# Two engines share the last rows, and all engines get new sequences: a one-core mix of a state-space convolution and a spectral filter

## The chip, the cores and the metric

The kernel runs on one core of one Trainium2 chip. The metric is device time in microseconds (us) of one execution, as the median of the timed runs. The engines are named as in the profile: PE is TensorE's matmuls and PEld its weight loads, DVE is VectorE, ACT is ScalarE, POOL is GpSimd, SP is SyncE, which here only issues DMAs. A `q` behind an engine's name (ACTq, SPq) means its instruction queue, for instance the issue of a DMA.

## What is computed

Two branches over 2048 positions and 640 channels are mixed by a gate for each position. Branch A convolves `u` along the positions with a kernel `K` that is a sum of 128 complex exponentials for each channel (computed by FFT in the reference). Branch B multiplies the two-dimensional spectrum of the same input by weights:

```
x = A_u
g = sigmoid((x * gate_w).sum(-1, keepdims=True))
a = irfft(rfft(u, 4096) * rfft(K, 4096))[:2048] + u * D_skip      # K = 2 Re sum_n C exp(A dt l)
b = irfft2(rfft2(x) * (w_r + 1j * w_i))
return g * a + (1 - g) * b
```

## The kernel before

All transforms are matmuls in float32 against tables, in stages of short transforms. The 640 channels are worked in four blocks `c` of 160.

- **Phase A** (`phase_a`, L575 to L643) transforms `u` (matmuls L532 and L546), writes the spectrum to HBM (`u_d`) and makes the gate.
- **The spectral filter** (the second half of `phase_a`, L659 to L782) reads that spectrum back in nine pairs of frequencies: transposes (L700), products with tables (L710, L764), the elementwise filter on VectorE, copies out of PSUM on ScalarE (L702, L717, L753, L768), and writes `s3e_d`.
- **Phases P and B** (L427 to L883) make the convolution kernel K in 40 tiles of 16 channels: matmuls L832 and L840, on ScalarE an exponential (L833) and two sines (L846 outer, L852 inner), products on VectorE (L860 to L862) and GpSimd (L865, L866), matmuls L876, a copy L882 and a write to `k_d`. Exponential and sine need different ScalarE tables; a tiny activation at L409 (`PRIME`) is put where the function changes, so that the table load stands there.
- **Phases C and D** (L876 to L1052) transform K (L532, L546), multiply with the spectrum of `u` (`us`, loaded at L960; L971 to L974), transform back (L988, copies L990 and L992), write the result to HBM (`s3_d`, for the last block `s3f_d`; issued by ScalarE's queue at L997 and L1000), load it back in another layout (`t3`, L1021 by SyncE), and make the last transform (`last`, L1030).

The last stage of a block has three chunks of 3, 3 and 2 rows (`CHUNKS`) for each of two halves `j`: 16 rows of 160 channels on 128 partitions. `last_e` makes branch B's part, times (1 - g), into `oe`. `last_c` makes branch A's part in PSUM, multiplies by g and adds `oe` into `ot`; the output leaves from `ot` (L1052). In the last block (`c == 3`) each row is one VectorE instruction (L1048) that multiplies and adds. Before these, eight matmuls at L1072 whose result nobody reads keep TensorE running. For the last block, `t3` is loaded in twelve pieces: four sets of partitions `y` (`t3[y::4]`), each of three chunks. Set 3 holds the last group of frequencies (written at L1000); set 2 needs also the odd frequency (written at L997).

The order of all work is written out by hand: the program is recorded as a numbered list of operations, and `ORDER` lists the numbers (`5846+10` is 5846 to 5855). Each engine runs its own operations in that order and waits where it must; DMAs are issued by the engine on which they are listed. Buffers are given to tiles in the same order. Numbers that matter below: 5787 to 5794 are the last eight matmuls of L988, 5795 is the copy behind them, 5796 and 5797 the last two writes at L1000, 5749 and 5750 those at L997. 5826 to 5837 are the twelve loads (three each for sets 0, 1, 2, 3). 5846 to 5853 is the first chunk's block of L1030 matmuls.

Two sorts of operations have no result that is used: `SPARE` is a count of fill matmuls (L406, 128 columns each), which the order puts where TensorE would stand still, and `PRIME` is the count of the tiny activations by function (Exp, Sin, Arctan, Ln, Sigmoid).

Of the kernel before, what the change touches and what calls it, by code (L numbers as in the profile page):

```python
# [15 lines left out]
ALU = mybir.AluOpType  # L16
# [926 lines left out]
def phase_d(tc, A, T, ctx, out):  # L943
# [95 lines left out]
    def last_c(c, a, n):  # L1039

        oe = oes.pop((c, a))
        p = last("p_c", lambda g: T.e3[c < 3], lambda g, r: t3s[c][r, 4 * a + n * g:4 * a + n * g + n], n)
        ot = o2.tile([128, 2, 3, 160], F32, tag="ot", name="ot")
        if c == 3:
            for j in range(2):
                for i in range(n):
                    x = 8 * j + a + i
                    V.scalar_tensor_tensor(out=ot[:, j, i], in0=p[:, j, i], scalar=T.gate[:, 0, x:x + 1], in1=oe[:, j, i], op0=ALU.mult, op1=ALU.add)  # L1048
        else:
            V.tensor_tensor(out=ot[:, :, 0:n], in0=p, in1=gate(0, a, n), op=ALU.mult)  # L1050
            G.tensor_tensor(out=ot[:, :, 0:n], in0=ot[:, :, 0:n], in1=oe[:, :, 0:n], op=ALU.add)
        (G if c < 2 else nc.sync).dma_start(out[c].rearrange("p (j a) d -> p j a d", j=2)[:, :, a:a + n], ot[:, :, 0:n])  # L1052
# [24 lines left out]
SPARE = (128, 278), (32, 0)  # L1077
PRIME = 23, 23, 1, 1, 1
# [97 lines left out]
```

## Time and profile before

| | |
|---|---|
| three timed runs | 535.62, 536.0, 543.41 us; median 536.0 |
| the profiled execution | 533.92 us, its span 531.9 |
| granted TensorE clock, mean | 0.993 |
| DMA moved in the span | 101.17 MB, 190 GB/s |
| TENSOR_TENSOR of VectorE in the last 36 us, 128x640 from PSUM (L971) | 0.82 us each |
| outputs issued by SyncE after 510 us (L1052) | 6, 3.0 to 4.8 us from issue to landing |

The profile's rows give the line, the engine, the operation, what it writes and reads, the shape and the count, then busy us and mean ns of one, then the idle time of the engine before them and what ended it. A row of a stretch (from:to) gives its length, the busy us of each engine with the number of instructions, the granted TensorE clock, the share of DMA time and GB/s. A float32 matmul leaves two records. A row of a chain or of a timeline begins with the start and the length in us.

### The profile page before, as it was taken

The numbers are of one execution on the slowest core, as the hardware profiler recorded it, in microseconds if no ns is written. First come the engines' busy times: TensorE is split into PE (matmuls) and PEld (weight loads), VectorE is DVE, ScalarE is ACT, GpSimd is POOL, SyncE is SP. The second block draws the span as 40 slices with busy tenths as digits, with TensorE's granted clock in tenths as the row PEclk, the third lists the DMA queues.
The fourth block names the chain that finished last, engine by engine and source line by source line (L and its number), as shares of the span: only waits on it lengthen the run. The fifth ranks groups of instructions, "written<-read, shape, count | busy, mean of one in ns | idle before, by whom it ended". The sixth has DMA issues, their size and how long they took to land. (4 is left out here: it accounts for less than half of the span.)

```text
span 531.9 us, 19458 instructions
## 1 busy us (share of the span) xinstructions
PE 499.3 (94%) x8600; PEld 409.5 (77%) x8600; DVE 397.6 (75%) x548; ACT 354.6 (67%) x505; POOL 226.1 (43%) x236
## 2 busy tenths in 40 slices
PE   8999999899999989999989999998999997999993
PEld 6899797788887878877768888886797886887740
DVE  5994236989899999598688696879575673767754
ACT  3787887699989877899969989966433242332210
POOL 1003213674766253746554525526431245337350
PEclk9999999999999999999989999999999999999998
DMA  8969526782313335132040231413997799799986
GB/s 318 361 199 339 171 81 215 250 256 84 101 67 110 125 103 170 46 118 70 30 147 32 67 110 52 127 55 123 358 338 240 247 374 390 261 321 311 340 266 234
DMA packets 58363, 101.17 MB, mean 190 GB/s; under 512 B 4980, under 2 KB 42136, under 8 KB 58248
## 3 DMA queue, kind: packets, MB, share of 16 engines
q1 hardware_dynamic: 34680, 67.82, 37.2%
q10 hardware_dynamic: 20368, 21.79, 12.3%
q0 software_dynamic: 3232, 10.33, 5.8%
q8 instruction: 67, 1.10, 0.8%
q14 instruction: 16, 0.13, 0.1%
HBM read 60.60 MB, written 39.65 MB: 188 GB/s over the span
## 5 line engine op out<-in xcount | busy, mean ns | idle before, releaser
L546 PE MATMUL psum<-sbuf,sbuf 128*64 128x160 f32 x1056 | 89.2, 308 | 6.5 <-ACT sbuf L536 2.7
L546 PEld LDWEIGHTS psum<-sbuf,sbuf 128*64 128x64 f32 x1056 | 72.7, 134 | 19.3 <-issue 6.5
L406 PE MATMUL psum<-sbuf 128*128 128x128 f32 x556 | 79.0, 287 | 0.0
L532 PE MATMUL psum<-sbuf,sbuf 128*64 128x128 f32 x1280 | 77.2, 274 | 0.2 <-issue 0.2
L406 PEld LDWEIGHTS psum<-sbuf 128*128 128x128 f32 x556 | 67.0, 192 | 11.3 <-issue 9.1
L532 PEld LDWEIGHTS psum<-sbuf,sbuf 128*64 128x64 f32 x1280 | 72.2, 137 | 3.8 <-issue 2.5
L710 PE MATMUL psum<-sbuf 64*128 64x161 f32 (+1 forms) x864 | 68.9, 305 | 4.3 <-DVE sbuf L771 2.2
L710 PEld LDWEIGHTS psum<-sbuf 64*128 64x128 f32 (+1 forms) x864 | 60.8, 182 | 9.4 <-DVE sbuf L771 2.3
L862 DVE TENSOR_TENSOR sbuf<-sbuf,psum 128x1024 f32<-128x1024 f32 x40 | 48.5, 1216 | 25.3 <-ACT psum L852 25.2
L833 ACT ACTIVATE sbuf<-psum 128x1024 f32<-128x1024 f32 (+1 forms) x80 | 60.9, 803 | 4.8 <-PE psum L832 3.1
L409 ACT ACT_TABLE_LOAD x48 | 61.6, 1283 | 0.8
L974 POOL TENSOR_TENSOR sbuf<-sbuf 128x320 f32<-128x320 f32 (+1 forms) x36 | 32.1, 893 | 68.3 <-DVE sbuf L972 57.3
L990 ACT COPY sbuf<-psum 128x640 f32<-128x640 f32 x32 | 21.9, 693 | 52.3 <-PE psum L988 36.1
L865 POOL TENSOR_TENSOR sbuf<-sbuf,sbuf 128x512 f32<-128x512 f32 x24 | 34.0, 1417 | 31.2 <-ACT sbuf L846 22.4
L579 ACT COPY sbuf<-psum 128x512 f32<-128x512 f32 (+2 forms) x58 | 35.3, 626 | 17.1 <-PE psum L532 11.7
L536 ACT COPY sbuf<-psum 128x512 f32<-128x512 f32 x40 | 23.9, 620 | 34.2 <-PE psum L532 22.8
L852 ACT ACTIVATE psum<-psum 128x1024 f32<-128x1024 f32 x40 | 40.3, 1008 | 9.3 <-PE psum L840 9.2
L876 PEld LDWEIGHTS psum<-sbuf 128*32 128x32 f32 x2560 | 37.9, 110 | 9.1 <-issue 7.1
L876 PE MATMUL psum<-sbuf 128*32 128x64 f32 x2560 | 44.4, 221 | 0.5 <-issue 0.4
L988 PEld LDWEIGHTS psum<-sbuf,sbuf 64*128 64x128 f32 x528 | 37.6, 186 | 6.8 <-issue 4.6
L988 PE MATMUL psum<-sbuf,sbuf 64*128 64x160 f32 x528 | 42.7, 305 | 0.1
L846 ACT ACTIVATE sbuf<-psum 128x1024 f32<-128x1024 f32 x40 | 40.7, 1017 | 2.8 <-PE psum L840 2.8
(133 smaller groups left out, 827.9 us busy)
## 6 DMA issues: line engine op xcount, KB each, us to landing
u_d<-sbuf SPq DMA_DIRECT2D x32, 320.0 KB, 4.2
sbuf<-u_d ACTq DMA_DIRECT2D x16, 640.0 KB, 6.7
s_d<-sbuf ACTq DMA_DIRECT2D x24, 320.0 KB, 5.8
sbuf<-s_d SPq DMA_DIRECT2D x6, 960.0 KB, 8.4
sbuf<-in_w_l SPq DMA_DIRECT2D x8, 644.0 KB, 4.1
sbuf<-u_d SPq DMA_DIRECT2D x8, 640.0 KB, 4.8
k_d<-sbuf SPq DMA_DIRECT2D x20, 256.0 KB, 2.3
sbuf<-k_d SPq DMA_DIRECT2D x8, 640.0 KB, 6.9
```

The source lines that it names most:

```text
L406: nc.tensor.matmul(spare[x:x + cols, i, :], c1[:, x:x + cols], c1[:, 128:256], start=True, stop=True)
L409: nc.scalar.activation(prime[0:1, i:i + 1], c1[0:1, 0:1], f)
L532: nc.tensor.matmul(p[64 * ri:64 * ri + 64, q // 4, 0:512].rearrange("p (h x) -> p h x", h=2)[:, :, 64 * (q % 4):64 * (q % 4) + 64], src[:, ...
L546: nc.tensor.matmul(p[64 * j:64 * j + 64, y, 160 * ro:160 * ro + 160], T.w2[:, x, ro, :], t1[:, x // 2 if x < 32 else K0 // 2, :, x % 2 if ...
L579: return (V.tensor_copy if T.dve and dst.home.name == "ut" else S.copy)(dst, src)
L710: P.matmul(p[:st.nl, c, 161 * i:161 * i + 161], src[r, k, x, 0:st.nl], td[r, w, k, :], start=k == 0, stop=k == 2)
L833: S.activation(ef[:, :, c:c + n], p[:, :, 0:n], AF.Exp)
L846: S.activation(sc.rearrange("p d v i -> p (d v i)"), p.rearrange("p j w -> p (j w)"), AF.Sin, scale=TWO_PI)
L852: S.activation(f, f, AF.Sin, scale=TWO_PI)
L862: V.tensor_tensor(out=x[:, 0].rearrange("p d (h j) -> p d h j", h=2), in0=e[:, :, 0:64].rearrange("p d (h j) -> p d h j", h=2), in1=cx.uns ...
L876: P.matmul(st.pb[32 * r:32 * r + 32, o, :], y[:, ri, 4 * qq + r, :], x[:, ri, 4 * qq + r, :], start=t % 2 + qq + 1 - ri == 0, stop=t % 2 * ...
L988: P.matmul(p[:, j, 160 * i:160 * i + 160], T.w3[r, pr, im, :], t2[r, h + i, im], start=im == 0, stop=im == 1)
```

## The change

In the last block, rows `i` = 0 and 1 of the second half `j` = 1 of each chunk, six of the 16, no longer run on VectorE. ScalarE multiplies them by the gate on the way out of PSUM (an activation with a scale for each partition), and GpSimd adds `oe`. Ten rows stay on VectorE.

```diff
@@ -1045,7 +1045,11 @@
             for j in range(2):
                 for i in range(n):
                     x = 8 * j + a + i
-                    V.scalar_tensor_tensor(out=ot[:, j, i], in0=p[:, j, i], scalar=T.gate[:, 0, x:x + 1], in1=oe[:, j, i], op0=ALU.mult, op1=ALU.add)
+                    if j and i < 2:
+                        S.activation(ot[:, j, i], p[:, j, i], AF.Copy, scale=T.gate[:, 0, x:x + 1])
+                        G.tensor_tensor(out=ot[:, j, i], in0=ot[:, j, i], in1=oe[:, j, i], op=ALU.add)
+                    else:
+                        V.scalar_tensor_tensor(out=ot[:, j, i], in0=p[:, j, i], scalar=T.gate[:, 0, x:x + 1], in1=oe[:, j, i], op0=ALU.mult, op1=ALU.add)
         else:
             V.tensor_tensor(out=ot[:, :, 0:n], in0=p, in1=gate(0, a, n), op=ALU.mult)
             G.tensor_tensor(out=ot[:, :, 0:n], in0=ot[:, :, 0:n], in1=oe[:, :, 0:n], op=ALU.add)
```

`SPARE` has 64 fill matmuls less and `PRIME` one sine less. `ORDER` is replaced as a whole:

```diff
-SPARE = (128, 278), (32, 0)
-PRIME = 23, 23, 1, 1, 1
+SPARE = (128, 214), (32, 0)
+PRIME = 23, 22, 1, 1, 1
...
-5682 5695+8 5570 5568 5673 5704 5683+8 5703 5706 5691 5707+8 5705 5693 5828 5692 5715 5799+8 5827 5826 5716 5740+2 5717+10 5743 5742 5745 5744 5728+8
-5727 5807 5746+2 5736 5752+8 5738 5737 5748 5761 5760 5764+8 5763 5571+8 5762 5773 5776+8 5772 5775 5774 5784 5829 5831 5579 5582+8 5786 5830 5787+8
-5785 5590 5580 5795 5593+8 5808+8 5750 5601 5796+2 5838+8 5602 5816 5749 5581 5591 5603 5835 5832 5836 5833 5837 5592 5834 5817+9 5846+10 5861+8 5857
-5856 5859 5858 5869 5860 5873 5870 5872 5876+8 5871 5874 5885 5875 5886+2 5884 5888
...
+5628 5447+2 5627 5650+8 5449 5637 5751 5658 5638+8 5659 5646 5662+8 5660+2 5647+2 5671 5674+8 5568 5670 5673 5570 5682 5695+8 5569 5672 5703 5799+8
+5704 5707+8 5807 5706 5827 5683+8 5705 5826 5715 5828 5719+8 5691 5717 5716 5693 5740+2 5727 5718 5692 5743 5571+8 5742 5745 5744 5752+8 5579 5761
+5580 5808+8 5760 5728+8 5762+2 5736 5764+8 5581 5816 5737+2 5582+8 5772+2 5746+2 5590 5829 5776+8 5775 5748 5830+2 5774 5591 5784 5593+8 5817+8 5785
+5601 5786+9 5749+2 5602 5825 5592 5795+2 5838+8 5797 5603 5832+6 5846+9 5863+8 5859 5855 5857 5860+2 5856 5858 5874 5880+8 5876 5871 5875 5862 5888
+5892 5890 5889 5893 5872 5891 5873 5878 5877 5894 5879
```

Up to 5856 the numbers mean the same in both. In the new list each of the six rows is two operations (ScalarE, then GpSimd: 5857 and 5858, 5859 and 5860 for the first chunk; 5873 to 5876 for the second, 5890 to 5893 for the third), the second chunk's matmuls are 5863 to 5870 and the third's 5880 to 5887, its outputs are 5862, 5879 and 5894, the fill is 5895 to 6108 (before: 5889 to 6166) and the tiny activations 6109 to 6156 (before: 6167 to 6215). Every engine's sequence changes, in the middle of the kernel too. In the end shown here, the old order of the last loads is 5835 5832 5836 5833 5837, an output (5592), 5834; the new one is 5592 and 5603, then 5832 to 5837 in order of number. The old order has three blocks of L1030 before 5787 that the lines above show from 5799 on; the new one has six.

135 rows, old and new, of the table ORDER are left out of this document.

## The prediction

> **What bounds the kernel now.** I read the page first, then the busy times by stage, then the last stage's chain and timeline. The profiled execution took 533.92 us around a span of 531.9; the three timed runs have a median of 536.0. I make the sum on the former and carry the difference over.
>
> ```profile
> span 531.9 us, 19458 instructions
> PE 499.3 (94%) x8600; PEld 409.5 (77%) x8600; DVE 397.6 (75%) x548; ACT 354.6 (67%) x505; POOL 226.1 (43%) x236
> ...
> L406 PE MATMUL psum<-sbuf 128*128 128x128 f32 x556 | 79.0, 287 | 0.0
> ...
> L409 ACT ACT_TABLE_LOAD x48 | 61.6, 1283 | 0.8
> ```
>
> TensorE (PE) looks full, but L406 is fill: 278 matmuls (two records each) of 79.0/278 = 0.284 us that no result uses. They stand where the sequence expects TensorE to wait. So the middle of the kernel must be read for ScalarE and TensorE together. I cut it at every fourth inner activation (L852, tiles 1, 5, 9 ... 37 and the last):
>
> ```profile
> core 0: us, PE busy (x) PEld busy (x) DVE busy (x) ACT busy (x) POOL busy (x), PEclk, DMA share, GB/s
> 76.70:113.70 37.00, 34.83 (x562) 27.93 (x559) 30.07 (x34) 29.16 (x39) 16.75 (x16) 1.00 0.67 221
> 113.70:147.50 33.80, 33.03 (x616) 27.59 (x616) 31.00 (x37) 32.84 (x45) 23.29 (x23) 1.00 0.38 123
> 147.50:167.60 20.10, 19.12 (x376) 15.86 (x374) 19.49 (x27) 17.55 (x24) 11.51 (x12) 1.00 0.29 98
> 167.60:215.70 48.10, 46.38 (x768) 38.41 (x768) 46.98 (x63) 37.10 (x50) 22.05 (x26) 1.00 0.39 119
> 215.70:237.30 21.60, 20.98 (x488) 16.78 (x485) 15.78 (x20) 21.23 (x29) 11.77 (x11) 1.00 0.25 79
> 237.30:261.90 24.60, 23.88 (x404) 19.18 (x403) 19.12 (x27) 23.68 (x33) 13.60 (x13) 1.00 0.17 55
> 261.90:290.70 28.80, 25.63 (x466) 20.87 (x464) 24.18 (x29) 24.67 (x35) 17.04 (x18) 0.94 0.28 87
> 290.70:315.70 25.00, 24.06 (x482) 19.78 (x480) 18.42 (x24) 23.53 (x33) 8.26 (x8) 1.00 0.21 69
> 315.70:361.60 45.90, 45.26 (x802) 38.11 (x798) 36.48 (x49) 37.94 (x54) 22.96 (x20) 1.00 0.31 92
> 361.60:374.10 12.50, 10.37 (x266) 7.97 (x268) 11.48 (x15) 7.74 (x11) 7.21 (x10) 1.00 0.36 119
> sum 297.40, PE 283.53 PEld 232.47 DVE 252.99 ACT 255.44 POOL 154.43; mean PE 28.35 PEld 23.25 DVE 25.30 ACT 25.54 POOL 15.44
> ```
>
> ScalarE is 94 to 98% busy in four of the ten stretches (the second, fifth, sixth, eighth) and idles in the others: 37.00 - 29.16 = 7.8 us in the first, 11.0 in the fourth, 8.0 in the ninth. After that come the convolution's stages, where TensorE and the DMA engines are full, and the end:
>
> ```profile
> 379.70:494.00 114.30, 110.22 (x1632) 92.96 (x1630) 75.26 (x109) 37.49 (x61) 45.26 (x49) 1.00 0.90 316
> 494.00:511.00 17.00, 15.53 (x208) 11.20 (x212) 13.28 (x19) 3.54 (x6) 6.63 (x7) 1.00 0.98 321
> ```
>
> Of the 131 us there TensorE idles 5.6. The matmuls in these stages are the same in both sequences, so a new order can win little in them. The last 20 us are a chain of waits:
>
> ```profile
> 509.56 0.59 ACTq L1000
> ...
> 510.19 0.73 ACTq L1000
> ...
> 511.74 1.19 ACTq L1000
> ...
> 512.97 4.40 DMA s3f_d<-sbuf
> ...
> 518.11 0.57 SPq L1021
> ...
> 523.86 1.04 PE psum L1030 x16
> ```
>
> The last write to HBM lands at 512.97 + 4.40 = 517.37 (call it W). Then SyncE issues the last six reloads, the three chunks' matmuls follow, then VectorE's rows and the last output:
>
> ```profile
> 517.45 3.17 SPq L1021 DMA_DIRECT2D sbuf<-s3f_d  x5
> 520.66 0.60 SPq L1052 DMA_DIRECT2D out<-sbuf  x1
> 521.31 0.62 SPq L1021 DMA_DIRECT2D sbuf<-s3f_d  x1
> 521.33 1.04 PE L1030 MATMUL psum<-sbuf,sbuf 64*32 64x480 f32 x16 [1.55 <-DVE sbuf L1037]
> 524.93 3.08 DVE L1048 SCALAR_TENSOR_TENSOR sbuf<-psum,sbuf,sbuf 128x160 f32<-128x160 f32 x10 [0.69 <-PE psum L1030]
> 525.89 0.77 PE L1030 MATMUL psum<-sbuf,sbuf 64*32 64x320 f32 x16 [0.99 <-issue]
> 528.04 0.53 SPq L1052 DMA_DIRECT2D out<-sbuf  x1
> ```
>
> The chunks start at W + 4.0, + 6.5 and + 8.5, the last output is issued at W + 10.7 and the span ends at W + 14.5. A row costs VectorE 3.08/10 = 0.31 us.
>
> **The change, part by part. The last rows.** Six rows leave VectorE: 6 x 0.31 = 1.85 us of its 4.9. Each becomes an activation from PSUM and a GpSimd add. Nearest rows:
>
> ```profile
> L992 ACT COPY sbuf<-psum 64x160 f32<-64x160 f32 x1 | 0.3, 287 | 1.5 <-PE psum L546 1.5
> L974 POOL TENSOR_TENSOR sbuf<-sbuf 64x160 f32<-64x160 f32 x1 | 0.5, 517 | 0.0
> L974 POOL TENSOR_TENSOR sbuf<-sbuf 128x320 f32<-128x320 f32 x4 | 3.6, 908 | 8.2 <-DVE sbuf L972 8.2
> ```
>
> So 0.29 us on ScalarE, and 0.52 on GpSimd, whose upper bound is the 320-wide 0.91. I take 0.52, the row of the same 160 elements. The per-row scale is not in the copy's row; its bounds are nothing and a second 0.29, and ScalarE has only six rows to make while VectorE makes ten, so nothing. In the new order the two adds of the second and third chunk queue on GpSimd behind each other, and the last two outputs on SyncE wait for them; nothing waits behind those.
>
> **The last reloads.** The old order interleaves partitions "3" and "2" of each chunk and puts an output (5592) ahead of the last load. The new one issues the three loads of "2" first. They need only the writes up to L997, which now go out ahead of the last two L1000, so they can land before W. After W remain three loads, at about W + 0.1, + 0.7 and + 1.3 (one per 0.63 us in the row of five) instead of six up to W + 3.9. Before, the first chunk's second load was issued at 518.11 and its matmuls began at 521.33, 3.2 us later; the third chunk's came 525.89 - 521.31 = 4.6 us after its last load. With 3.1 to 4 us from issue to matmuls, since fewer loads fly together, the chunks can start at W + 3.2, + 4.3 and + 5.3. VectorE's four rows of chunk one run W + 4.3 to 5.5, then it waits for chunk three at W + 6.1, and ends near W + 7.9; ScalarE ends at W + 6.9; GpSimd, six adds of 0.52 from W + 4.7 with short waits, at W + 8.2. The last output goes at W + 8.3 instead of + 10.7: 2.4 us won. With 0.91 per add GpSimd ends at W + 10.2 and 0.4 is won.
>
> **What is put ahead of W.** Before the last eight L988 matmuls the new order has six L1030 blocks where the old had three:
>
> ```profile
> L1030 PE MATMUL psum<-sbuf,sbuf 64*32 64x480 f32 x96 | 6.2, 571 | 4.4 <-DVE sbuf L1037 1.6 <-DMA sbuf<-s3f_d 1.5 <-DMA sbuf<-s_d 1.4
> L1030 PE MATMUL psum<-sbuf,sbuf 64*32 64x320 f32 x48 | 2.3, 440 | 1.0 <-issue 1.0
> ```
>
> A block of 16 records is 6.2/6 = 1.04 us or 2.3/3 = 0.77. One long and two short ones are 2.6 us more. They cover the 1.4 us wait on the s_d reload, so W comes 1.2 later; the first L1000 after the last copy took 1.19 where the two before it took 0.59 and 0.73, and without an L997 still to come behind it I give 0.5 back. W moves by +0.7 (between 0 and +2.6), and the end of the kernel wins 2.4 - 0.7 = **1.7 us** (-2.2 to +2.4).
>
> **Table load.** PRIME has one Sin less, so one pair of load and tiny activation goes: 1.28 + 0.20 us.
>
> ```profile
> 208.52 1.28 ACT L409 ACT_TABLE_LOAD   x1
> ...
> 209.82 0.20 ACT L409 ACTIVATE sbuf<-sbuf 1x1 f32<-1x1 f32 x1
> ```
>
> It counts by ScalarE's busy share of the ten stretches, 255.44/297.40 = 0.86: **1.3 us** (0 to 1.5). The Trainium skill (ScalarE: Activation LUTs, What ACT_TABLE_LOAD costs) adds a drain of 1380 ns to each load. Here the activation starts 0.02 us after the load, so no drain shows behind it; by the page this term would be (1.28 + 1.38 + 0.20) x 0.86 = 2.5 us, an estimate, and the sum below 7.5.
>
> **Fill and order in the middle.** Counted between the same L852 in both sequences, the fill changes by -12, -14, -4, -16, +9, -7, -12, +5, -15, +2 (sum -64), 18.2 us of TensorE. F-stage work (L700, L710, L764) per tile stays the same to within 24 instructions, so the mix of stages hardly moves. A stretch can shorten by no more than its removed fill, and by no more than ScalarE's idle time in it. In the four full stretches that gives 1.0 - 2.5 + 0.9 - 1.4 = -2.0 us. In the other six at most 3.4 + 1.1 + 4.5 + 3.4 + 4.2 - 0.6 = 16.0. Both ends: none of it, or 14.0 in all. The long fill runs stand where ScalarE is full (131 of 278 in the four stretches, 105 of 297 us), and in the idle stretches ScalarE waits mostly for real matmuls; so I take a third of the 16.0: 5.3 - 2.0 = **3.3 us** (-2.0 to 14.0).
>
> **Sum:** 1.7 + 1.3 + 3.3 = 6.3 us. 533.92 becomes 527.6 as profiled, and 536.0 becomes **529.7** as timed.
>
> **The rivals.** *A really shorter middle.* If removed fill means that real work moved up, all 14.0 us come: 14.0 + 1.3 + 1.7 = 17.0, 519.0 us. For it speak 297.4 - 255.4 = 42 us of idle ScalarE; against it the unchanged mix. It is past 2% from 10.7 - 3.0 = 7.7 us in the middle.
>
> *The clock falls (the other side).* Less fill leaves TensorE idle:
>
> ```profile
> 268.70:272.10 3.40, 1.22 (x18) 1.09 (x20) 3.39 (x5) 2.50 (x4) 2.38 (x4) 1.00 0.28 77
> 272.10:275.50 3.40, 3.40 (x28) 2.78 (x25) 2.00 (x2) 0.75 (x1) 0.00 (x0) 0.50 0.87 211
> ```
>
> A stretch with 1.22 us of work in 3.40 was followed by 3.4 us at clock 0.50, which costs 1.7 us. Suppose the middle gains nothing from its order and the clock falls in five more places: 536.0 - 1.7 + 5 x 1.7 = 542.8 us. It decides from the second place on. Against it: 18.2 us spread over 300 is one fill in 4.7 us, and the old kernel fell only once. The Trainium skill (TensorE: Matmul & The Clock Gate, Why this matters for your kernels) wants a gap of about 3 us before the clock drops; by that this rival costs nothing. The rows disagree: 2.2 us idle sufficed.
>
> *The end gains nothing* (GpSimd adds at 0.91, or W later by all 2.6 us): 536.0 - 4.6 = 531.4.
>
> **How the numbers follow.** Forecast 0.42 (its own range, with -1 to +7.4 us from the middle, 525.6 to 534), shorter middle 0.30, clock 0.18, no gain at the end 0.10. A measurement tells about 2%, 10.7 us. The shorter middle is past it (0.30 faster); the clock rival is past it from eight places on, for which I keep 0.10; the rest, 0.42 + 0.10 + 0.08 = 0.60, is within. The range is 519.0 to 541.0: down to the whole of the first rival, up to four falls of the clock.
>
> **What would show it.** Right: the last output about 8.3 us after the last s3f_d write lands, VectorE's rows no longer last, GpSimd adds near 0.52; the last L876 some 4 to 5 us sooner; clock 1.00 in the middle but for a place or two. Wrong: an s3f_d reload issued after W waiting on L997, adds near 0.9, several rows of clock 0.5 to 0.8, or a middle shorter by over 8 us.

## The result, and the profile after

The kernel after takes 541.47 us, the median of 20 runs (537.34 to 547.92), against 536.52 for the kernel before in 20 runs beside it. The ratio is 1.0103, with a 95% interval of 1.0077 to 1.0129: slower by 1.0%, which is less than 2%, but the interval excludes no change. The time lies 0.5 us past the upper end of the range. (Ratios leave disturbed runs out, so one can differ a little from the quotient of two medians.) The profiled execution took 543.57 us around a span of 541.6, 9.7 us more than that of before, where the medians lie 4.95 apart. Much of what follows is about that difference.

The head of the page and the two rows of fill and table loads, as shown of before:

```profile
span 541.6 us, 19212 instructions
PE 489.8 (90%) x8472; PEld 400.2 (74%) x8472; DVE 399.5 (74%) x542; ACT 355.1 (66%) x509; POOL 227.4 (42%) x242
...
L406 PE MATMUL psum<-sbuf 128*128 128x128 f32 x428 | 64.2, 291 | 0.0
...
L409 ACT ACT_TABLE_LOAD x47 | 60.3, 1283 | 0.8
```

The work went as announced: 14.8 us less fill, one table load less, and TensorE busy for 9.5 us less in a span that is 9.7 us longer. So TensorE stands still for 19 us more in this execution. Its longest waits in the first 400 us of after (us in total, times, longest):

```profile
PE psum L832 <- DMA sbuf<-par_d: 3.8, 1, 3.8
PE psum L876 <- DVE sbuf L860: 2.5, 2, 2.1
PE psum L840 <- DVE sbuf L773: 2.4, 2, 2.2
...
PE psum L876 <- issue: 2.2, 1, 2.2
PE psum L532 <- DMA sbuf<-in_u_l: 2.1, 1, 2.1
PE psum L700 <- DVE sbuf L579: 2.1, 1, 2.1
```

Before had one wait of 2 us or more there (2.2 us, L710 on VectorE's L771), and its first L832 waited 1.2 us for the same DMA. Five stretches of 3.4 us that hold a wait from this list, each with the stretch behind it (from:to, length, busy us of each engine, granted clock, DMA share, GB/s):

```profile
59.20:62.60 3.40, 1.25 (x20) 1.03 (x22) 0.00 (x0) 1.31 (x3) 0.00 (x0) 1.00 0.40 96
62.60:66.00 3.40, 3.40 (x36) 3.15 (x32) 0.00 (x0) 0.81 (x2) 0.00 (x0) 0.51 0.00 0
103.60:107.00 3.40, 1.38 (x17) 1.19 (x18) 3.40 (x4) 1.64 (x3) 2.55 (x3) 1.00 0.87 311
107.00:110.40 3.40, 3.40 (x25) 2.03 (x22) 3.40 (x6) 1.07 (x2) 1.79 (x2) 0.50 0.75 237
236.70:240.10 3.40, 1.25 (x64) 1.00 (x55) 3.40 (x5) 2.54 (x4) 0.30 (x1) 1.00 0.62 236
240.10:243.50 3.40, 3.40 (x70) 2.55 (x60) 2.38 (x4) 1.91 (x3) 0.00 (x0) 0.51 0.15 61
277.70:281.10 3.40, 1.30 (x12) 1.09 (x12) 3.40 (x6) 1.87 (x3) 1.85 (x3) 1.00 0.13 39
281.10:284.50 3.40, 3.40 (x56) 2.65 (x58) 1.24 (x2) 2.10 (x4) 2.49 (x2) 0.50 0.62 188
373.30:376.70 3.40, 1.43 (x24) 1.34 (x25) 1.73 (x2) 0.59 (x1) 1.08 (x3) 1.00 0.66 228
376.70:380.10 3.40, 3.40 (x28) 2.23 (x26) 0.00 (x0) 1.82 (x3) 1.68 (x3) 0.50 0.83 264
```

Read the second column and the clock together. With 1.25 to 1.43 us of matmuls in 3.40, the next 3.4 us ran at half clock. That happened five times; in the profile of before it happened once before its end, at 272.1. (The sixth wait of 2 us or more in the list, of L532 at 6.6 us, was followed by no fall: it left 1.92 and 2.82 us of matmuls in the two stretches in which it lies.) Four more falls cost at most 4 x 1.7 = 6.8 us of the 9.7. The landmarks fit that only roughly: tile 5 is 5.5 us late (113.7 to 119.2), the last L876 5.8 (379.7 to 385.6), the last L988 8.5 (510.9 to 519.4). The 2.7 us between the last two came at full clock, and no run explains them.

The end of after, timeline:

```profile
524.45 3.80 SPq L1021 DMA_DIRECT2D sbuf<-s3f_d  x6
530.30 2.38 PE L1030 MATMUL psum<-sbuf,sbuf 64*32 64x480 f32 x48 [1.82 <-DMA sbuf<-s3f_d]
531.37 0.68 DVE L1052 SCALAR_TENSOR_TENSOR sbuf<-psum,sbuf,sbuf 128x160 f32<-128x160 f32 x2 [11.19 <-PE psum L1030]
531.51 2.02 ACT L1049 ACTIVATE sbuf<-psum,sbuf 128x160 f32<-128x160 f32 x6 [9.79 <-PE psum L1030]
531.99 1.49 POOL L1050 TENSOR_TENSOR sbuf<-sbuf 128x160 f32<-128x160 f32 x3 [11.16 <-ACT sbuf L1049]
532.23 2.43 DVE L1052 SCALAR_TENSOR_TENSOR sbuf<-psum,sbuf,sbuf 128x160 f32<-128x160 f32 x8 [0.18 <-ACT sbuf L1049]
533.02 2.71 SPq L1056 DMA_DIRECT2D out<-sbuf  x3
533.43 1.00 POOL L1050 TENSOR_TENSOR sbuf<-sbuf,sbuf 128x160 f32<-128x160 f32 x2
534.39 0.52 POOL L1050 TENSOR_TENSOR sbuf<-sbuf 128x160 f32<-128x160 f32 x1
```

The last write to s3f_d lands at 525.90 (W). The chunks follow each other without a gap from W + 4.4, the last output is issued at 535.14 = W + 9.24 instead of W + 10.7 before, and an add takes 0.52 us. Yet the span ends at 541.59 = W + 15.7, where before it ended at W + 14.5. What closes it is neither VectorE nor an output. The closing instructions, first of before, then of after (duration min/median/max in ns, first and last start in us):

```profile
L1172 POOLq EVENT_SEMAPHORE  x4: 17/17/17, 531.2 to 531.8; - x4
L1172 POOLq DRAIN  x3: 46/102/9637, 512.7 to 531.6; - x3
L1172 SPq DRAIN  x3: 7/7/13, 531.1 to 531.4; - x3
```

```profile
L1176 POOLq EVENT_SEMAPHORE  x4: 17/17/17, 540.8 to 541.5; - x4
L1176 POOLq DRAIN  x3: 46/102/7223, 533.6 to 541.3; - x3
L1176 SPq DRAIN  x3: 7/7/7, 538.7 to 541.1; - x3
```

GpSimd closes with a DRAIN. In before it is issued at 512.66 and ends at 512.66 + 9.64 = 522.30, 5.89 us after GpSimd's last add (516.41) and long before SyncE has seen the last output (531.1). In after the last add ends at 534.91, the DRAIN at 533.58 + 7.22 = 540.80, again 5.89 us later; SyncE was done at 538.7. So GpSimd ends the kernel, 2.1 us late.

### The profile page after: what moved, and what is told of

The parts are those of the page before. It is cut to its first block, busy times and chain, and to the rows that moved or that the text cites. A ratio compares the mean times of both kernels' runs of the same rounds, so it can differ in the third digit from the quotient of the medians.

```text
span 541.6 us, 19212 instructions
## 1 busy us (share of the span) xinstructions
PE 489.8 (90%) x8472; PEld 400.2 (74%) x8472; DVE 399.5 (74%) x542; ACT 355.1 (66%) x509; POOL 227.4 (42%) x242
## 5 line engine op out<-in xcount | busy, mean ns | idle before, releaser
L546 PE MATMUL psum<-sbuf,sbuf 128*64 128x160 f32 x1056 | 91.1, 310 | 3.7 <-issue 1.6
L546 PEld LDWEIGHTS psum<-sbuf,sbuf 128*64 128x64 f32 x1056 | 73.2, 136 | 16.3 <-issue 6.5
L532 PE MATMUL psum<-sbuf,sbuf 128*64 128x128 f32 x1280 | 79.1, 277 | 2.2 <-DMA sbuf<-in_u_l 2.1
L532 PEld LDWEIGHTS psum<-sbuf,sbuf 128*64 128x64 f32 x1280 | 73.4, 139 | 6.3 <-DMA sbuf<-in_u_l 3.5
L710 PE MATMUL psum<-sbuf 64*128 64x161 f32 (+1 forms) x864 | 68.1, 304 | 1.5 <-ACT sbuf L846 0.6
L710 PEld LDWEIGHTS psum<-sbuf 64*128 64x128 f32 (+1 forms) x864 | 60.9, 182 | 6.3 <-ACT sbuf L833 1.1
L406 PE MATMUL psum<-sbuf 128*128 128x128 f32 x428 | 64.2, 291 | 0.0
L406 PEld LDWEIGHTS psum<-sbuf 128*128 128x128 f32 x428 | 52.8, 193 | 10.6 <-issue 8.4
L876 PE MATMUL psum<-sbuf 128*32 128x64 f32 x2560 | 45.2, 223 | 5.5 <-DVE sbuf L860 2.5
L866 POOL TENSOR_TENSOR sbuf<-sbuf,sbuf 128x512 f32<-128x512 f32 x24 | 33.1, 1382 | 38.7 <-ACT sbuf L846 33.5
L876 PEld LDWEIGHTS psum<-sbuf 128*32 128x32 f32 x2560 | 38.8, 112 | 13.8 <-issue 11.5
L972 DVE TENSOR_TENSOR sbuf<-psum,sbuf 128x640 f32<-128x640 f32 (+1 forms) x36 | 28.1, 781 | 24.2 <-PE psum L546 13.1
L865 POOL TENSOR_TENSOR sbuf<-sbuf,sbuf 128x512 f32<-128x512 f32 x24 | 33.0, 1379 | 24.8 <-ACT sbuf L846 24.8
```

What stands on the lines that cost most here:

```text
L406: nc.tensor.matmul(spare[x:x + cols, i, :], c1[:, x:x + cols], c1[:, 128:256], start=True, stop=True)
L532: nc.tensor.matmul(p[64 * ri:64 * ri + 64, q // 4, 0:512].rearrange("p (h x) -> p h x", h=2)[:, :, 64 * (q % 4):64 * (q % 4) + 64], src[:, ...
L546: nc.tensor.matmul(p[64 * j:64 * j + 64, y, 160 * ro:160 * ro + 160], T.w2[:, x, ro, :], t1[:, x // 2 if x < 32 else K0 // 2, :, x % 2 if ...
L710: P.matmul(p[:st.nl, c, 161 * i:161 * i + 161], src[r, k, x, 0:st.nl], td[r, w, k, :], start=k == 0, stop=k == 2)
L866: G.tensor_tensor(out=y[:, 0], in0=e[:, :, 64:96], in1=sc[:, 1], op=ALU.mult)
L876: P.matmul(st.pb[32 * r:32 * r + 32, o, :], y[:, ri, 4 * qq + r, :], x[:, ri, 4 * qq + r, :], start=t % 2 + qq + 1 - ri == 0, stop=t % 2 * ...
```

## The experiments

Two theories stood against each other. **The clock:** the time goes to the new order's long waits of TensorE, and the fill that would have covered them is gone. **The end:** it goes to the rows on GpSimd, whose closing DRAIN now comes last. The rival to the first was the one of the prediction: less fill by itself. Where a run's mean clock is used, it is turned into time at half clock, 2 x (1 - clock) x span, averaged over the runs that its ratio uses: 19.4 us for after, and 11.6 for before in each of two groups of experiments (the runs of before beside after have no clock on record). Half of a difference is taken as its cost in us, an estimate. Runs of one and the same kernel bear it out: over all 193 with a clock on record, a us more at half clock goes with 0.53 us more of time (0.46 to 0.60); over the 163 that the ratios use, with 0.41 (0.33 to 0.49). But half clock behind the last matmul of a kernel, where TensorE has nothing left to do, costs nothing, and it is counted too: in the profiles 3.8 us in before and 4.5 in after. The changes to `ORDER` that go with each edit are left out below.

**One half of the change each.** The old order with only the six rows moved:

```diff
-                    V.scalar_tensor_tensor(out=ot[:, j, i], in0=p[:, j, i], scalar=T.gate[:, 0, x:x + 1], in1=oe[:, j, i], op0=ALU.mult, op1=ALU.add)
+                    if j and i < 2:
+                        S.activation(ot[:, j, i], p[:, j, i], AF.Copy, scale=T.gate[:, 0, x:x + 1])
+                        G.tensor_tensor(out=ot[:, j, i], in0=ot[:, j, i], in1=oe[:, j, i], op=ALU.add)
+                    else:
+                        V.scalar_tensor_tensor(out=ot[:, j, i], in0=p[:, j, i], scalar=T.gate[:, 0, x:x + 1], in1=oe[:, j, i], op0=ALU.mult, op1=ALU.add)
```

> The old sequences with only the six rows moved to ScalarE and GpSimd (an activation and an add stand where each VectorE row stood; fill, tiny activations and all else as before). Theory 'GpSimd's drain': GpSimd's closing drain ends 5.9 us after its last add, so the end of the kernel is set by it: last add about 9.5 us after the last s3f_d write lands, end of the span at about +16.2 instead of +14.5, ratio to before 1.002 to 1.004. Rival 'the split is good for itself' (the prediction's): VectorE is relieved of 1.85 us, ratio 0.998 to 1.000, the end of the span still about 3.9 us behind the last output's issue.

Measured: 538.01 us against 534.4, ratio 1.0051 (1.0013 to 1.0090). The last add ended at 534.96, GpSimd's closing semaphore came at 540.89, 5.93 us later and 3.0 us after SyncE was done (537.9). That is about the size of the 2.7 us lost, whose interval is 2 us to either side. Half clock rose from 11.6 to 14.1 us, but in the profile 8.3 us of it lie behind the last matmul, against 3.8 in before, so the clock may have no part in it. The new order with all 16 rows on VectorE is the reverse of that edit, applied to after:

> The new sequences with all 16 rows on VectorE again (each row stands where its activation stood). Theory 'GpSimd's drain': the end comes about 3.9 us behind the last output instead of 6.5, and the rows end 1 us later; net 1 to 1.5 us faster than the changed kernel, ratio to before 1.006 to 1.009. Theory 'the loss is in the order and the clock': most of the 1% stays, ratio over 1.005. Rival 'the split is the loss': ratio 1.000 or under.

Measured: 539.56 us, ratio 1.0087 (1.0049 to 1.0126), with four falls of the clock up to 526.7 us and one more at the very end. (17.3 - 11.6)/2 = 2.9 of 4.7 us is clock; the other 1.8 has an interval of about 2.1 to either side and stays open. Both halves lose; the order seems to lose more, but the two intervals overlap.

**The waits refilled.** After, with 35 fill matmuls put back at five of its waits: 12 ahead of the first L832 (into that tile's own PSUM), 5 ahead of an L700, 6 each ahead of an L840 and two L876.

```diff
-SPARE = (128, 214), (32, 0)
+SPARE = (128, 237), (32, 0)
...
+            for _ in range(12):
+                nc.tensor.matmul(T.pe0[:, 0, 0:128], c1[:, 0:128], c1[:, 128:256], start=True, stop=True)
...
+            if t + c == 0:
+                T.pe0 = p
```

> The changed kernel with 35 more fill matmuls in the five places where TensorE stood still for 2 us and more ahead of a fall of the clock: 12 ahead of the first L832 (into that tile's own PSUM, which it overwrites), 5 ahead of an L700, 6 each ahead of an L876, an L840 and an L876. Theory 'the clock': the five stretches at clock 0.5 go, each worth up to 1.7 us, so 4 to 8.5 us faster than the changed kernel, ratio to before 0.995 to 1.003. Rival 'the waits themselves': filling a wait doesn't shorten it and the fallen clock was hidden by other waits; ratio stays 1.008 to 1.012 though the clock stays up.

Measured: 536.64 us, ratio 1.0023 (0.9989 to 1.0057), half clock 10.5 us instead of the 19.4 of after. Its longest waits in the first 400 us (its lines stand four further down: L836 is L832 of after, L880 is L876):

```profile
PE psum L836 <- ACT sbuf L837: 2.8, 8, 0.7
PE psum L577 <- DVE sbuf L572: 1.6, 1, 1.6
PE psum L880 <- DVE sbuf L864: 1.2, 2, 0.8
```

No single wait is over 1.6 us, and the clock did not fall before 513.9. 35 matmuls of 64.2/214 = 0.30 us, 10 us more of TensorE work, gave back 0.8% of the time (the two intervals do not overlap). By the clock it should be (19.4 - 10.5)/2 = 4.5 us, which is 0.8%. The end is untouched by it: GpSimd's last add at 525.83, its semaphore at 531.76.

**Less fill by itself.** The old order with 214 fill matmuls instead of 278, each run of fill shortened in proportion:

```diff
-SPARE = (128, 278), (32, 0)
+SPARE = (128, 214), (32, 0)
```

> The old sequences with 214 fill matmuls instead of 278, every run of fill shortened in proportion; nothing else. Theory 'the clock': TensorE stands still more, the clock falls in two to four more places, 2 to 6 us slower, ratio 1.004 to 1.011. Rival 'fill only covers': TensorE's idle time grows by up to 18 us, the clock stays, ratio 0.998 to 1.002. If the fill had delayed real work, it would be faster: ratio under 0.998.

Measured: 533.58 us, ratio 0.9974 (0.9933 to 1.0016), half clock 12.6 us, 1.0 more than in before. So the theory, as this expectation put it, falls, and the prediction's rival ("less fill leaves TensorE idle") with it. TensorE stood still for 31.2 of the first 400 us here, almost as long as the 33.9 in the profile of after, against 18.4 in before. It is not how much fill there is but where the long waits are. This kernel still has its wait of 2.2 us (L710), and in its profile the clock held there:

```profile
266.69:270.10 3.41, 2.21 (x80) 1.36 (x74) 3.41 (x2) 3.30 (x7) 3.39 (x5) 1.00 0.30 82
270.10:273.51 3.41, 2.04 (x30) 1.99 (x32) 3.38 (x5) 1.34 (x2) 1.12 (x2) 1.00 0.39 118
```

The wait lies across the border of two stretches, and each keeps over 2 us of matmuls. In before the same wait lay inside one (1.22 of 3.40), and the clock fell.

**A late GpSimd by itself.** The old kernel with one more add on GpSimd. It reads the first row of the last chunk and ran right behind VectorE's last row (531.59); its result is read by nothing.

```diff
+            if a == 6:
+                G.tensor_tensor(out=oe[:, 0, 0], in0=ot[:, 0, 0], in1=oe[:, 0, 0], op=ALU.add)
```

> The old kernel with one GpSimd add of one row (128x160) more, behind the last VectorE row; its result is read by nothing, and the output's DMA doesn't wait for it. Theory 'GpSimd's drain': its closing drain ends 5.9 us behind this add, so GpSimd's last semaphore comes 5.9 us after it and the span ends about 6.7 us after it, 2.5 to 3 us later than before: ratio 1.004 to 1.006. Rival 'the adds' own waits': nothing waits for this add, so nothing changes, ratio 0.998 to 1.002.

Measured: 541.19 us against 534.45 in four runs, ratio 1.0118 (1.0062 to 1.0174). Its closing instructions:

```profile
L1174 POOLq EVENT_SEMAPHORE  x4: 17/17/17, 538.2 to 538.8; - x4
L1174 POOLq DRAIN  x3: 46/102/6438, 531.7 to 538.6; - x3
L1174 SPq DRAIN  x3: 7/7/7, 534.6 to 538.4; - x3
```

One add of 0.52 us, ended at 532.24, holds the kernel open until 538.2, 5.9 us after it and 3.6 after SyncE was done. That is 0.7% of the time. The ratio is larger than that, and larger than either theory said. Of the 17.8 - 11.6 = 6.2 us more at half clock, 3.7 lie behind the last matmul in the profile and cost nothing; the other 2.5 are worth some 1.3 us. What is left of the 6.3 us lies within the interval of 3 us to either side. The mechanism is shown, its size from the trace and not from the ratio.

**Both mended.** The refilled kernel with only the first chunk's two rows off VectorE, so that GpSimd ends earlier:

```diff
-                    if j and i < 2:
+                    if a == 0 and j and i < 2:
```

> The refilled new sequences (the third experiment) with only the first chunk's two rows on ScalarE and GpSimd, the other 14 on VectorE. GpSimd's last add comes some 2.5 us earlier, so its drain ends before the last output lands. Theories 'clock' and 'drain' together: the end of the span about 4 us behind the last output's issue and 1.5 to 2 us sooner than in the third experiment: ratio to before 0.996 to 1.000. Rival 'the split is worth its six rows': no gain on the third experiment, ratio 1.001 to 1.004.

Measured: 533.24 us against 534.45, ratio 0.9972 (0.9929 to 1.0014), half clock 7.1 us. GpSimd and SyncE now end together:

```profile
L1180 POOLq EVENT_SEMAPHORE  x4: 17/17/17, 532.3 to 532.9; - x4
...
L1180 SPq DRAIN  x3: 7/7/7, 532.2 to 532.5; - x3
```

It has the lowest ratio of the variants with the new order, clear of that of after, but not of 1. The refilled kernel with all 16 rows on VectorE:

```diff
-                    if j and i < 2:
-                        S.activation(ot[:, j, i], p[:, j, i], AF.Copy, scale=T.gate[:, 0, x:x + 1])
-                        G.tensor_tensor(out=ot[:, j, i], in0=ot[:, j, i], in1=oe[:, j, i], op=ALU.add)
-                    else:
-                        V.scalar_tensor_tensor(out=ot[:, j, i], in0=p[:, j, i], scalar=T.gate[:, 0, x:x + 1], in1=oe[:, j, i], op0=ALU.mult, op1=ALU.add)
+                    V.scalar_tensor_tensor(out=ot[:, j, i], in0=p[:, j, i], scalar=T.gate[:, 0, x:x + 1], in1=oe[:, j, i], op0=ALU.mult, op1=ALU.add)
```

> The refilled new sequences with all 16 rows on VectorE. By 'drain', compared with the third experiment: the last output is issued 1.5 to 2 us later, the end of the span comes 2.5 us closer behind it: 0.5 to 1 us faster, ratio to before 0.999 to 1.002. If the split had no cost at the end, this would be 1.7 us slower than the third experiment, ratio 1.004 to 1.007.

Measured: 535.95 us, ratio 0.9989 (0.9947 to 1.0030). W is at 512.97, the last output at W + 10.3, the end at W + 14.5, as in before: in these two profiles the new order of the last loads by itself wins 0.4 us for the output and nothing for the end. The first chunk's rows alone end at W + 13.6.

**The old order with its own long waits filled**, 6 fill matmuls ahead of the L710 of 2.2 us and 5 ahead of an L840:

```diff
-SPARE = (128, 278), (32, 0)
+SPARE = (128, 289), (32, 0)
```

> The old sequences with 11 more fill matmuls in the two longest waits of the middle: 6 ahead of the L710 that waited 2.2 us at 271 us (behind which the clock fell), 5 ahead of the L840 that waited 1.7 us at 364 us. Theory 'the clock': the stretch at clock 0.5 near 272 us goes, 1 to 1.7 us faster, ratio 0.996 to 0.999. Rival 'the fallen clock was hidden': ratio 0.999 to 1.002 with the clock at 1.00.

Measured: 534.90 us, ratio 1.0022 (0.9982 to 1.0062), half clock 9.7 us: no gain to be seen, though its profile shows no fall before 525.7. The theory's 1 to 1.7 us did not come, but they are no larger than the interval of 2 us to either side. The profile also shows a long wait that cost nothing by the clock. Its first L832 waited 3.1 us, and still:

```profile
PE psum L832 <- DMA sbuf<-par_d: 3.1, 1, 3.1
```

```profile
58.10:61.51 3.41, 1.69 (x26) 1.22 (x22) 0.00 (x0) 2.86 (x5) 0.00 (x0) 1.00 0.58 183
61.51:64.92 3.41, 2.01 (x39) 1.44 (x43) 0.12 (x1) 1.59 (x3) 0.00 (x0) 1.00 0.03 7
```

**The first wait moved instead of filled.** The kernel with both mended, without its 12 fill matmuls ahead of the first L832: that pair, its table load and exponential go behind 24 matmuls L532 and 20 L616.

```diff
-544+2 6176+12 2253+2 546+16 6129 2255 564+8 562 750+20 572 563 2256+2
+544+18 564+8 562 750+20 572 563 2253+2 6129 2255+3
```

> The sixth experiment (refilled new sequences, only the first chunk's two rows off VectorE), but the first two L832 matmuls with their table load and exponential are moved behind the 24 L532 and 20 L616 matmuls that followed them, in place of the 12 fill matmuls ahead of them. So the wait for the parameter load (3.8 us in the changed kernel) is covered by real work. Theory 'only the clock cost' of this wait: filling had already won all there was, ratio 0.995 to 1.001 as in the sixth. Theory 'the wait itself delays the middle': up to 3 us more, ratio 0.990 to 0.995.

Measured: 536.34 us, ratio 1.0064 (1.0025 to 1.0104): a miss for both theories. Its single profile is short (a span of 527.7, no fall before 522.4), yet the runs are not. Between its ratio and that of the kernel it was made from lie 0.9%, 4.9 us. (8.8 - 7.1)/2 = 0.9 us of that is clock; the rest was not explained.

## Why the prediction was wrong, step by step

**The clock decided, and it was held for a rival at 0.18.** Its price of 1.7 us a fall, and even its total (five falls, 542.8), stood near what was measured. Its reason, "less fill leaves TensorE idle", was too coarse, since thinner fill in the old order cost nothing. The argument against it, "one fill in 4.7 us", is the step that failed: it averages over 300 us, and one single wait decides. Four waits of 2.05 to 2.2 us are new in after: their cover had gone, and fill put back there took the falls away. The fifth, of 3.8 us on a parameter load, is partly chance: that load also kept L832 waiting for 2.0 and 3.1 us in two profiles of the old order (the late add and the filled waits). The total is luck in part, too. With the 0.7 us that after has more behind its last matmul taken off, the runs show (19.4 - 11.6 - 0.7)/3.41 = 2.1 more falls than before, not five: some 3.5 us. The profiled execution caught five, four more than that of before, and so the two profiles lie 9.7 us apart where the medians lie 4.95 apart.

**"The end of the kernel wins 1.7 us".** The pieces were nearly right: adds of 0.52, last output at W + 9.2 (forecast + 8.3; the chunks began 1.2 us later than forecast: the six reloads could start only at 524.45, so the first that needs the last write went out at W + 0.5 instead of W + 0.1 and took 3.8 us to land). The step that failed is the sentence after the sum, "nothing waits behind those". GpSimd's closing DRAIN does: it ends 5.9 us after the last add. Counted from W the end moved by +1.2 instead of -2.4, and the DRAIN was to be seen in the trace of before, among the rows that no engine counts as busy. Whether W itself moved by the forecast 0.7 stays open. From the last matmul of the tiles to W, profiles without a fall in between show 136.6 to 137.6 us in the old order, 136.0 and 137.7 in the new one refilled, and 140.3 in after.

**"Table load" and "Fill and order in the middle", 4.6 us.** This gain is not in the times. Profiles without a fall before 400 us show the last matmul of the tiles at 377.0 to 377.9 us in the new order refilled, and at 377.3, 377.6 and 380.6 in the old one (only the rows moved, thin, filled): 1.0 us between the means, with 3.3 among the old ones. The ratios show less still. Refilled with the rows on VectorE, the new order has 0.9989, 0.6 us less than before, and its clock alone, (11.6 - 8.2)/2 = 1.7 us, explains more than that. At equal clock it would be some 1 us slower, with 2 us to either side, so a gain of 4.6 us is out for this order. Taking a third of an upper bound gave a number where the profile gave none. Why the shorter fill let nothing move up is not shown.

Put together: 3.5 us of clock, 1.2 of the end, and about nothing from the middle make 4.7 us, of 4.95 between the medians and 5.5 by the ratio. That they close so well is partly luck. Before took 536.5 us beside after, but 534.4 in the groups from which its clock is taken, so the clock's share may be off by a us or two. Of the listed signs, the adds near 0.52 came true. So did "several rows of clock 0.5 to 0.8", listed as a sign of being wrong. No sign was listed that could have caught the DRAIN.

## What to carry to other kernels

Judge an order of work by the longest single wait of TensorE, not by the sum of its idle time: here 35 fill matmuls at five long waits brought back 0.8%, and taking away 64 spread over the kernel cost nothing that could be seen. Look at an engine's closing instructions before giving it the last work of a kernel; here GpSimd's last operation should end 6 us before SyncE sees the last output. And where two profiles differ by more than the medians do, count the events that only some executions have.

## What the runs showed of the hardware

**The clock is decided in stretches of 3.413 us on a fixed grid.** The five falls of after begin at 62.6, 107.0, 240.1, 281.1 and 376.7 us, which is 0, 13, 52, 64 and 92 times 3.413 us behind the first. In the eleven profiles, leaving out the last 14 us of each, 14 such stretches at full clock had at most 1.50 us of matmuls, and each was followed by one at half clock; of seven with 1.51 to 1.68 us two were; of some 1600 with more, none. So a wait of 2.1 us costs up to 1.7 us if it falls inside one stretch, and nothing by the clock if it lies across a border. Where the grid lies differs from run to run. The wait of L840 of 2.2 us lay inside one stretch in after, and the clock fell; in the new order with all rows on VectorE the same wait lay across a border, with 2.39 and 2.28 us of matmuls in the two stretches, and the clock held. By the idle time of 3.41 - 1.50 = 1.91 us that makes a fall, a wait of 2.1 us falls in about (3.41 + 2.1 - 2 x 1.91)/3.41 = 0.5 of the runs, one of 3.8 us in all: 1 + 4 x 0.5 = 3.0 for after and some 0.5 for before, an estimate, against 2.1 more by the runs. The Trainium skill (TensorE: Matmul & The Clock Gate, What's actually happening) gives the window as 3413 ns and free-running, and the traces agree. Its rule of thumb that gaps up to about 3 us are safe (Why this matters for your kernels) does not hold here: 2.05 us was enough.

**GpSimd's closing DRAIN** ended 5.89 us after GpSimd's last operation in all eleven profiles, whether that was one added row, the last of six rows or an add of 640 or 960 columns.

**A scaled copy from PSUM on ScalarE** (128x160) took 0.39 us alone, and six in a row 2.02 us, 0.34 each. No table load stood ahead of them: the last of after began at 351.5 us.
